# A hand-written order with decay columns made on TensorE against one annealed list of single steps, with Strassen's seven products in nine pairs

## The chip, the cores and the metric

The kernel runs on one core of one Trainium2 chip. The metric is the device time of one execution in microseconds (us). The core has a matrix engine (TensorE, PE in the profile; its weight loads are PEld), a vector engine (VectorE, DVE), an activation engine (ScalarE, ACT), a general engine (GpSimd, POOL) and a queue engine (SyncE, SP). Each works through its own instructions in order and waits on semaphores. TensorE writes to PSUM, eight banks of 128 x 512 float32.

## The reference

Two stages, float32 in and out. First a linear attention with decay for 4 batches, 8 heads, 768 tokens and head size 48, then a feed-forward layer of width 2048 on the 3072 tokens of 384 channels:

```python
for t in range(S):
    cur = einsum('bhd,bhe->bhde', u * k[t], v[t])
    y[t] = einsum('bhd,bhde->bhe', r[t], state + cur)
    state = w * state + einsum('bhd,bhe->bhde', k[t], v[t])
x = y.transpose(0, 2, 1, 3).reshape(3072, 384)
h = x @ w_in                      # 384 x 2048
out = maximum(0.01 * h, h) @ w_out   # 2048 x 384
```

## The kernel before

The tokens are cut into 24 stages of 128 (six to a batch), and two stages make a pair (12 pairs). A stage's attention is done in matrix form, the feed-forward layer stage by stage for the first four stages and pair by pair behind. Everything is bfloat16 in SBUF, with sums in PSUM. The steps have letters, which the lists and the texts use (n is a stage, m a pair):

- `r`, `k`, `v` n: loads of a stage, by DMA issued on POOL with a cast (L217); `wi`, `wo` g: quarters of w_in and w_out (L227, L231). Stage 0's r and k come over SP and ACT as float32.
- `P` n (prep): r and k times powers of the decay, on VectorE, from `qtab` and `ktab`, which ScalarE makes from w. From stage 8 on it also issues the transposition as a DMA on SP. `T` n (turn): for stages 0 to 7 the transposition as eight matmuls with `ident` (L367), copied out by ScalarE (L378).
- `A` n: the 128x128 products of r and k of all heads, two PSUM banks (L391). `M` n: their mask, on VectorE (L409; from stage DIAG on one predicated copy of 1024, L401, over the tile that `Q` laid out).
- The bonus u on the diagonal has two routes. Below stage DIAG (8): `X` n (VectorE, L329) and matmuls with `wu` inside `K` (L421), then `Q` scales v (L337), and three matmuls of `Y` add it (L513). From DIAG on: `Q` n computes one number per token and head with three VectorE operations (L342, L344, L346), and GpSimd multiplies `ident` by it into the two halves of `at` (L354).
- `K` n: the stage's update of the state (L425); below stage 8 the state carried over is added by a matmul with `ident` (L430), behind by VectorE in `S` (L478). `S` n: times the decay (L475, L480).
- `Y` n: attention output, from `at` and the state (L508), copied out as `xT`.
- `G` n.g, `J` m.j: parts of the first product for a stage (L541, four columns of blocks) or a pair (L558, two), each in one bank, with the leaky ReLU on ScalarE (L546, L564).
- `H` n, or `g2`: second product of a stage, 16 matmuls of 384 columns (L575). For pairs in SEVEN, `g2_seven` makes a pair's second product as Strassen's seven: seven times eight matmuls of 192 columns (L639), from four sums of halves of gT (`g_sum`, VectorE, L613) and of w_out (`w_sum`, L595). Products share banks: ScalarE keeps (`keep`, L647) and VectorE adds (`plus`, L670) between them.
- `C`, `W`: decay and bonus as columns. `C` turns the rows w and w*u by 16 + 8 one-column matmuls (L449, L450), ScalarE takes logarithms, VectorE casts `wu`; `W` makes the table `wl`. `U`: u over all partitions. `F` x: x matmuls of ones whose results nobody reads.

ORDER lists the steps up to pair 3 by hand, LOADS the first loads; then a loop over pairs 3 to 11 emits, for each pair, its first product, the attention of the stages two pairs on, and the second product of the pair before. Loads from stage 8 on wait for a J two pairs back (`pace`). Banks go round in the order of emission (`next_bank`).

Of the kernel before, what the change touches and what calls it, by code (L numbers as in the profile page):

```python
# [12 lines left out]
L = 128  # L13
# [10 lines left out]
FIRST, EARLY = 6, 2  # L24
LOADS = """r1 k1 r2 k2 wi0 id v1 r3 tri k3 v2 wi1 k4 r4 v3 wi2 k5 r5 r6 k6 v4 v5 k7 wi3 r7 v6 v7 wo3 wo2 wo1 wo0"""
ORDER = """
C W P0 P1 F1 T0 T1 P2 A0 X0 M0 A1 K0 T2 Q0 X1 Y0 A2 S0 M1 K1 X2 G0.0 Q1 P3 S1 Y1 T3 K2 M2 G1.0 X3 A3 U G0.1 S2 G1.1 Q2 M3 Y2 K3 P4
T4 Q3 G2.0 G2.1 G0.2 S3 G2.2 G1.2 Y3 P5 A4 P6 X4 M4 T5 X5 G3.0 K4 Q4 A5 S4 T6 G3.1 K5 G3.2 Y4 M5 L8 Q5 Y5 P7 A6 G1.3 J2.0 J2.1 T7
M6 X6 X7 K6 J2.2 J2.3 A7 S6 J2.4 J2.5 L9 Q6 G2.3 G0.3 J2.6 M7 L10 J2.7 L11 G3.3 K7 S7 P8 Q7 Q8 P9 H0 Q9 K8 H1 P10 L12 K9 H2 S8 S9
Y6 Y7 A8 A9 P11 M8 H3 M9 L13  # L30
# [90 lines left out]
def bass_rwkv5_eagle__then__act_leaky_relu_kernel(  # L121
# [17 lines left out]
    TURNED, DIAG = 8, 8  # L139
    SEVEN = (8,9,10,11)  # L140
# [17 lines left out]
    tcol = SB("tcol", [128, 1], FP32)  # L158
# [3 lines left out]
    wu_row = SB("wu_row", [1, HD])  # L162
# [6 lines left out]
    ku = [SB(f"ku{i}", [128, HD]) for i in range(2)]  # L169
    rku = [SB(f"rku{i}", [128, HD]) for i in range(2)]  # L170
    s_tok = [SB(f"s_tok{i}", [128, H], FP32) for i in range(2)]
# [5 lines left out]
    sum_t = [SB(f"sum_t{i}", [128, NP, 2 * D]) for i in range(2)]  # L177
# [41 lines left out]
    def load_stage(n, pace=()):  # L219
        for which in "krv":  # L220
            load_one(n, which, pace)
# [12 lines left out]
    def row(h):  # L234
# [5 lines left out]
    load_first("k")  # L240
    add("act", lambda: A.preload_act_table_set("natural_log_exp_and_others"))
    add("pool", lambda: G.iota(tcol[:, :], pattern=[[0, 1]], base=0, channel_multiplier=1,
                               allow_small_or_imprecise_dtypes=True), W=["tcol"])
    load_one(0, "v")
    add("dve", lambda: V.memset(one_row[:, :], 1.0), W=["one_row"])
    add("dve", lambda: V.memset(ones[:, :], 1.0), W=["ones"])
# [11 lines left out]

    ps_w, key_w = next_bank()

    def identity():
        add("pool", lambda: G.affine_select(ident[:, :], ones[:, 0:128], pattern=[[1, 128]], compare_op=ALU.is_equal,
                                            fill=0.0, base=0, channel_multiplier=-1), R=["ones"], W=["ident"])

    def triangle():
        add("pool", lambda: G.affine_select(mask[:, :], ones[:, 0:128], pattern=[[1, 128]], compare_op=ALU.is_ge,
                                            fill=0.0, base=-1, channel_multiplier=-1), R=["ones"], W=["mask"])

    for name in LOADS.split():
        if name == "id":  # L270
            identity()
        elif name == "tri":
            triangle()
        elif name[:2] == "wi":
            load_win(int(name[2:]))
        elif name[:2] == "wo":
            load_wout(int(name[2:]))
        else:
            load_one(int(name[1:]), name[0])

    add("dve", lambda: V.tensor_scalar(kexp[:, :], tcol[:, :], -1.0, float(MID - 1), ALU.mult, ALU.add),
        R=["tcol"], W=["kexp"])
    add("dve", lambda: V.tensor_scalar(qexp[:, :], tcol[:, :], 1.0, float(-MID), ALU.mult, ALU.add),
        R=["tcol"], W=["qexp"])
    add("dve", lambda: V.memset(v_sb[:, :, :].rearrange("p n (h e) -> p (n h) e", e=E)[:, :, D:E], 0.0), W=["v0"])
    add("dve", lambda: V.tensor_tensor(wu_row[:, :], w_row[:, :], u_row[:, :], ALU.mult),
        R=["w_row", "u_row"], W=["wu_row"])
# [11 lines left out]
    at_bank, kv_bank = {}, {}  # L299
# [10 lines left out]
    def prep(n):  # L310
        iq = n % NQK
        if n >= TURNED:
            both = rk_sb[:, n % NRK, :, :].rearrange("p w (h d) -> p (w h) d", d=D)
            by = tab[:, :, :].rearrange("p w (h d) -> p (w h) d", d=D)
            add("dve", lambda: V.tensor_tensor(qk[iq][:, :, 0:D], both, by, ALU.mult),
                R=[("r", n % NRK), ("k", n % NRK), "qtab", "ktab", ("qk0", iq)], W=[("qp", iq), ("kp", iq)])
            add("sp", lambda: SP.dma_start_transpose(tp[n % NTP][:, :, :],
                                                     qk[iq][:, :, :].rearrange("p h e -> p (h e)")),
                R=[("kp", iq), ("qp", iq), ("qk0", iq)], W=[("tp", n % NTP, 0), ("tp", n % NTP, 1)],
                dma=f"tp{n % NTP}")  # L320
            return
# [10 lines left out]
    def prep2(n):  # L332
        i2, iv = n % 2, n % NVS
# [7 lines left out]
        else:  # L341
            add("dve", lambda: V.tensor_tensor(ku[i2][:, :], k_of(n), u_tab[:, :], ALU.mult),  # L342
                R=[("k", n % NRK), "u_tab"], W=[("ku", i2)])
            add("dve", lambda: V.tensor_tensor(rku[i2][:, :], r_of(n), ku[i2][:, :], ALU.mult),  # L344
                R=[("r", n % NRK), ("ku", i2)], W=[("rku", i2)])
            add("dve", lambda: V.tensor_reduce(s_tok[i2][:, :], hd(rku[i2][:, :]), AX.X, ALU.add),  # L346
                R=[("rku", i2)], W=[("s", i2)])
            diag_tile(n)

    def diag_tile(n):  # L350
        ia = n % NAT
        for hh in range(2):
            s_of = s_tok[n % 2][:, :].rearrange("p (m two) -> p two m", two=2)[:, hh, :]
# [3 lines left out]
                R=["ident", ("s", n % 2)], W=[("at", ia, hh)])  # L357

    def turn(n):
        it, iq = n % NTP, n % NQK  # L360
        for half in ((0, 1) if n == 0 else (1, 0)):
# [12 lines left out]
            if n == 0 and half == 1:  # L374
                add("dve", lambda dst=dst, ps_t=ps_t: V.tensor_copy(dst, ps_t[:, :]),
                    R=[key], W=[("tp", it, half)])
            else:
                add("act", lambda dst=dst, ps_t=ps_t: A.activation(dst, ps_t[:, :], AF.Copy),  # L378
                    R=[key], W=[("tp", it, half)])

    def a_mm(n):
        it = n % NTP
        if n >= DIAG and taken[0] % 8 == 7:
            taken[0] += 1
# [12 lines left out]
    def a_mask(n):  # L397
        if n >= DIAG:
# [7 lines left out]
            return  # L406
        for hh in range(2):
            part = at_bank[n][hh][0][:, :].rearrange("p (m i) -> p m i", i=128)
            add("dve", lambda hh=hh, part=part: V.tensor_tensor(  # L409
                at[n % NAT][:, hh, :, :], part, mask[:, :].unsqueeze(1).to_broadcast([128, NP, 128]), ALU.mult),  # L410
                R=[at_bank[n][hh][1], "mask"], W=[("at", n % NAT, hh)])

    def kv_mm(n):
        iq = n % NQK
        ps_kv, key = kv_bank[n] = next_bank()
        live, carried = n % NC < NC - 1, n < DIAG and n % NC > 0
# [24 lines left out]
    def decay_columns():  # L441
        ps_c, key_c = next_bank()

        def emit():
            for hh in range(2):
                for p in range(NP):
                    c0 = (2 * p + hh) * D
                    rows = slice(64 * hh, 64 * hh + D)
                    PE.matmul(ps_c[rows, p:p + 1], w_row[:, c0:c0 + D], one_row[:, 0:1], start=True, stop=True)  # L449
                    last = PE.matmul(ps_c[rows, NP + p:NP + p + 1], wu_row[:, c0:c0 + D], one_row16[:, 0:1],  # L450
                                     start=True, stop=True)
            return last

        add("pe", emit, R=["one_row", "one_row16", "w_row", "wu_row"], W=[key_c, "wcols"])
        for hh in range(2):
            rows = slice(64 * hh, 64 * hh + D)
            add("act", lambda rows=rows, hh=hh: A.activation(wcol[rows, :], ps_c[rows, 0:NP], AF.Ln),
                R=[key_c], W=[f"wcol{hh}"])
            add("dve", lambda rows=rows, hh=hh: V.tensor_copy(
                wu[rows, :, hh:hh + 1].rearrange("p m o -> p (m o)"), ps_c[rows, NP:2 * NP]),  # L460
                R=[key_c, f"wcol{hh}", "wu"], W=[f"wu{hh}"])

    def decay_table():
        for hh in range(2):
            rows = slice(64 * hh, 64 * hh + D)
            add("act", lambda rows=rows, hh=hh: A.activation(
                wl[rows, :, hh * D:hh * D + D], wcol[rows, :].unsqueeze(2).to_broadcast([D, NP, D]), AF.Exp,
                scale=float(L)), R=[f"wcol{hh}", "wl"], W=[f"wl{hh}"])

    def state(n):  # L470
# [3 lines left out]
        if n % NC == 0 or n < DIAG:  # L474
            add("dve", lambda: V.tensor_tensor(new[:, :, :], kv, wl[:, :, :], ALU.mult),  # L475
                R=[key, "wl0", "wl1"], W=[("st", (n + 1) % NT)])
        else:
            add("dve", lambda: V.tensor_tensor(sum_t[n % 2][:, :, :], kv, st[n % NT][:, :, :], ALU.add),  # L478
                R=[key, ("st", n % NT)], W=[("sum", n % 2)])
            add("dve", lambda: V.tensor_tensor(new[:, :, :], sum_t[n % 2][:, :, :], wl[:, :, :], ALU.mult),  # L480
                R=[("sum", n % 2), "wl0", "wl1"], W=[("st", (n + 1) % NT)])
# [133 lines left out]
    def g2_seven(m):  # L615
        ig, i2 = m % NG, m % 2
        final = m == NST // 2 - 1
        banks = [next_bank() for _ in range(4 if final else 3)]
# [3 lines left out]
        def product(where, left, right, first, last):  # L622
            ps_o, key = banks[where]
# [19 lines left out]
            add("pe", emit, R=reads, W=[key])  # L643
# [30 lines left out]
        landed = []  # L674
        if not final:
            product(0, (0, 0), (top, one), True, False)
            keep(0, 0)
            product(1, 0, 0, True, False)
            keep(1, 1)
            product(0, 1, 1, False, False)  # L680
            keep(0, 2)
            product(2, (0, 1), (low, one), True, True)
            plus(2, 0, 0, 0)
            product(0, 2, 2, False, False)
            plus(0, 1, 1, 1)
# [132 lines left out]
```

## Time and profile before

| | |
|---|---|
| median of 3 runs | 171.15 us (171.03 to 171.33) |
| the profiled execution | 171.27 us, its span 169.5 us |
| TensorE busy | 163.1 us, 2203 matmuls |
| VectorE, ScalarE, GpSimd busy | 114.9, 93.3, 103.8 us |
| first product (L541, L558) | 13.0 and 54.5 us |
| second product plain, in sevens (L575, L639) | 43.3 us; 22.4 us in four groups |
| POOL-issued loads (queue q0) | 10.03 MB in 76512 packets |

The profile's span runs from the first instruction to the last; 1.77 us of the profiled execution's time lie around it. Busy times of TensorE count a matmul from its start to its modelled end, so neighbours overlap; start-to-start differences tell more. The chain of waits goes back from the last instruction to what released it.

### The profile page before, as it was taken

What the parts mean: (1) busy time and instruction counts of PE and PEld (TensorE: products, weight loads), DVE (VectorE), ACT (ScalarE), POOL (GpSimd) and SP (SyncE); (2) the same over time, 40 slices, a digit from 0 to 9 for tenths busy, and PEclk for the clock granted to TensorE, in tenths of its full rate; (3) what the DMA queues carried; (4) which work ended last, traced back from release to release, by engine and by line L of the source; (5) the groups of instructions that cost most, each with busy time, mean ns of one, the idle gap of its engine ahead of it and who ended that gap; (6) DMA issues with size and microseconds to landing.
All of it is one profiled execution on the core that took longest, in us unless ns stands there. A gap on an engine that the chain in (4) does not pass through costs nothing.

```text
span 169.5 us, 5112 instructions
## 1 busy us (share of the span) xinstructions
PE 163.1 (96%) x2203; PEld 129.1 (76%) x2203; DVE 114.9 (68%) x211; ACT 93.3 (55%) x176; POOL 103.8 (61%) x117
## 2 busy tenths in 40 slices
PE   6799999999999999999999999999999999999992
PEld 1577898889656876876866867867867899898991
DVE  7699766752998869379289299099199976053272
ACT  4752888789122852842933934824834836829320
POOL 7999999990379799791992995974506500000000
PEclk9999999999999999999999999999999999999999
DMA  5999999999999989999699499599107102011032
GB/s 95 117 155 159 170 155 171 194 185 145 126 167 197 167 50 126 214 73 114 172 74 156 130 74 154 135 106 205 51 0 173 48 4 93 4 40 55 4 115 70
DMA packets 99258, 19.66 MB, mean 116 GB/s; under 512 B 92322, under 2 KB 99236, under 8 KB 99236
## 3 DMA queue, kind: packets, MB, share of 16 engines
q0 software_dynamic: 76512, 10.03, 90.9%
q1 hardware_dynamic: 21682, 9.11, 25.6%
q8 instruction: 17, 0.28, 0.7%
q10 hardware_dynamic: 1042, 0.20, 0.6%
q14 instruction: 5, 0.04, 0.1%
HBM read 20.45 MB, written 4.72 MB: 148 GB/s over the span
## 4 chain that ended last, share of the span: by engine, by line
PE 93%; POOL 4%; ACT 1%; issue 1%; DVE 0%; DVEq 0%; POOLq 0%
PE ps_all L558 31%; PE ps_all L575 25%; PE ps_all L639 11%; PE ps_all L541 7%; PE ps_all L508 7%; PE ps_all L391 4%; PE ps_all L367 3%; PE ps_all L425 3%; POOL rk_sb L217 2%; PE ps_all L513 1%; ACT tp L378 1%; POOL v_sb L217 1%; PE ps_all L430 1%; PE ps_all L421 1%; POOL w_in_sb L227 0%
## 5 line engine op out<-in xcount | busy, mean ns | idle before, releaser
L558 PE MATMUL ps_all<-xT,w_in_sb 128*128 128x256 bf16 x480 | 54.5, 273 | 0.0
L354 POOL TENSOR_TENSOR at<-ident,s_tok 128x512 bf16<-128x512 bf16 x32 | 35.0, 1121 | 29.0 <-DVE s_tok L346 29.0
L558 PEld LDWEIGHTS ps_all<-xT,w_in_sb 128*128 128x128 bf16 x480 | 46.7, 98 | 6.1
L564 ACT ACTIVATE gT<-ps_all 128x512 bf16<-128x512 f32 x80 | 47.7, 597 | 5.8 <-PE ps_all L558 1.2
L575 PE MATMUL ps_all<-w_out_sb,gT 128*128 128x384 bf16 x256 | 43.3, 326 | 0.0
L575 PEld LDWEIGHTS ps_all<-w_out_sb,gT 128*128 128x128 bf16 x256 | 24.4, 98 | 15.9
L401 DVE CAST_PREDICATED at<-mask,ps_all 128x1024 bf16<-128x1024 uint16 x16 | 18.8, 1219 | 20.6 <-PE ps_all L391 20.6
L581 ACT ACTIVATE out_sb<-ps_all 128x384 f32<-128x384 f32 x16 | 7.8, 490 | 38.4 <-PE ps_all L575 38.4
L217 POOL DMA_DIRECT2D v_sb<-in_v_dram x24 | 22.6, 945 | 0.4 <-issue 0.4
L217 POOL DMA_DIRECT2D rk_sb<-in_k_dram x23 | 21.6, 941 | 0.0
L217 POOL DMA_DIRECT2D rk_sb<-in_r_dram x23 | 21.3, 929 | 0.0
L670 DVE TENSOR_TENSOR out_sb<-ps_all,snap 128x192 f32<-128x192 f32 x13 | 4.4, 355 | 15.1 <-PE ps_all L639 14.5
L344 DVE TENSOR_TENSOR rku<-rk_sb,ku 128x384 bf16<-128x384 bf16 x16 | 13.8, 861 | 0.6
L528 ACT ACTIVATE xT<-ps_all 128x384 bf16<-128x384 f32 x24 | 11.0, 490 | 5.1 <-PE ps_all L508 3.0
L541 PE MATMUL ps_all<-xT,w_in_sb 128*128 128x128 bf16 x192 | 13.0, 225 | 0.0
L541 PEld LDWEIGHTS ps_all<-xT,w_in_sb 128*128 128x128 bf16 x192 | 11.8, 101 | 0.5 <-issue 0.3
L409 DVE TENSOR_TENSOR at<-ps_all,mask 128x512 bf16<-128x512 f32 x16 | 10.2, 682 | 2.2 <-PE ps_all L391 2.2
L546 ACT ACTIVATE gT<-ps_all 128x512 bf16<-128x512 f32 x16 | 9.6, 599 | 3.8 <-PE ps_all L541 3.1
L508 PE MATMUL ps_all<-at,v_sb 128*32 128x128 bf16 x384 | 11.4, 228 | 0.0
L378 ACT ACTIVATE tp<-ps_all 128x512 bf16<-128x512 f32 x15 | 8.2, 596 | 3.7 <-PE ps_all L367 3.7
L508 PEld LDWEIGHTS ps_all<-at,v_sb 128*32 128x32 bf16 x384 | 8.4, 99 | 2.2 <-issue 0.5
L508 PE MATMUL ps_all<-tp,st 128*32 128x128 bf16 x240 | 9.8, 223 | 0.0
(80 smaller groups left out, 197.2 us busy)
## 6 DMA issues: line engine op xcount, KB each, us to landing
out_dram<-out_sb SPq DMA_DIRECT2D x22, 192.0 KB, 2.6
v_sb<-in_v_dram POOLq DMA_DIRECT2D x24, 96.0 KB, 5.5
rk_sb<-in_r_dram POOLq DMA_DIRECT2D x23, 96.0 KB, 5.2
rk_sb<-in_k_dram POOLq DMA_DIRECT2D x23, 96.0 KB, 4.6
w_in_sb<-in_moe_w_in_dram POOLq DMA_DIRECT2D x4, 384.0 KB, 7.0
w_out_sb<-in_moe_w_out_dram POOLq DMA_DIRECT2D x4, 384.0 KB, 10.9
out_dram<-out_sb SPq DMA_DIRECT2D x4, 96.0 KB, 1.7
tp<-qk SPq DMA_TRANSPOSE x16, 4.4
```

The lines of the kernel that those rows point to most:

```text
L217: add("pool", lambda: G.dma_start(dst, src), R=pace, W=[key], dma=f"{which}{n}")
L344: add("dve", lambda: V.tensor_tensor(rku[i2][:, :], r_of(n), ku[i2][:, :], ALU.mult), R=[("r", n % NRK), ("ku", i2)], W=[("rku", i2)])
L354: add("pool", lambda hh=hh, s_of=s_of: G.tensor_tensor(at[ia][:, hh, :, :], ident[:, :].unsqueeze(1).to_broadcast([128, NP, 128]), s_of.un ...
L401: add("dve", lambda: V.copy_predicated(at[n % NAT][:, :, :, :].rearrange("p two m i -> p (two m) i"), mask[:, :].bitcast(mybir.dt.uint16). ...
L409: add("dve", lambda hh=hh, part=part: V.tensor_tensor(at[n % NAT][:, hh, :, :], part, mask[:, :].unsqueeze(1).to_broadcast([128, NP, 128]) ...
L508: last = PE.matmul(ps_y[32 * q:32 * q + 32, 128 * s:128 * s + 128], a, m, start=first_mm and (s == 0 or n >= DIAG), stop=last_mm and n >= ...
L528: add("act", lambda: A.activation(xT[m % NX][:, :, 128 * half:128 * half + 128], ps_y[:, 0:HD].rearrange("p (s t) -> p s t", t=128), AF.Copy),
L541: last = PE.matmul(ps_g[:, 128 * f:128 * f + 128], w_in_sb[:, s, 128 * fb:128 * fb + 128], xT[ix][:, s, t], start=s == 0, stop=s == NSL - 1)
L558: last = PE.matmul(ps_g[:, 256 * f:256 * f + 256], w_in_sb[:, s, 128 * fb:128 * fb + 128], xT[ix][:, s, :], start=s == 0, stop=s == NSL - 1)
L564: add("act", lambda: A.activation(gT[ig][:, 2 * j:2 * j + 2, :].rearrange("p f t -> p (f t)"), ps_g[:, :], AF.Prelu, alpha=0.01), R=[key], ...
L575: last = PE.matmul(ps_o[:, 0:HD], gT[ig][:, s, 128 * half:128 * half + 128], w_out_sb[:, s, :], start=s == 0, stop=s == NFB - 1)
L639: done = PE.matmul(ps_o[:, 0:NH], lhs[:, s, :], rhs[:, s, :], start=first and s == 0, stop=s == HF - 1, skip_group_check=not (first and last))
```

## The change

The loop and LOADS go. One list, ORDER, names every load and every step; pairs' sums and products become single steps: `B` m.i a sum of gT, `V` i a sum of w_out, `Z` m.k a product of the seven with its keep, add or store. `I` x skips x banks. Loads have no pace. SEVEN holds pairs 3 to 11. DIAG goes from 8 to 6; the state is carried by a matmul for stages below CARRY (3) only. The decay and bonus columns come by four DMAs from w and u. `ident` and `mask` come from VectorE, from a ramp that POOL makes. `P` from stage 4 on is one operation for r and k. `M` n.how can take a half over ScalarE (bits 1, 2) or both halves in one operation (4). `ku` and `s_tok` have four buffers, `rku` is gone, the sums of states have four.

```diff
-FIRST, EARLY = 6, 2
-LOADS = """r1 k1 r2 k2 wi0 id v1 r3 tri k3 v2 wi1 k4 r4 v3 wi2 k5 r5 r6 k6 v4 v5 k7 wi3 r7 v6 v7 wo3 wo2 wo1 wo0"""
+EARLY = 3
 ORDER = """
-C W P0 P1 F1 T0 T1 P2 A0 X0 M0 A1 K0 T2 Q0 X1 Y0 A2 S0 M1 K1 X2 G0.0 Q1 P3 S1 Y1 T3 K2 M2 G1.0 X3 A3 U G0.1 S2 G1.1 Q2 M3 Y2 K3 P4
...
+wi0 r1 I3 F4 F2 I4 P0 I4 k1 C v0 r2 k2 T0 I1 r3 k3 v1 k5 v2 I4 F2 P1 A0 W r5 T1 X0 M0.4 F2 P2.0 K0 U Q0 T2 S0 A1 Y0 P3.0 X1 wi3 T3 X2 k4 A2 v3 r4 I3 r7 k7 M1.4 wi2 K1 wi1 S1 Q1 G0.0 k6 r6 v4 I3 I4 I4 K2 P5 Q2 M2.1 A3 M3.3 X3 Y1 T5 I3 G0.3 S2 Y2 G1.0 K3 P4 Q3 G1.3 T4 S3 v6 G2.3 v5 G2.0 Y3 k8 r8 P7 X5 A4 Q7 M4.0 A5 X4 G2.2 G3.2 wo3 wo0 M5.2 G3.3 v7 wo1 G1.1 wo2 Q6 G3.1 G0.2 T7 K4 G2.1 Q4 G1.2 Y4 P6 K5 S4 Q5 T6 G3.0 Y5 A7 A6 G0.1
...
+Q8 K7 r11 k10 I4 Y6 r10 Y7 k11 I2 v9 J2.0 S7 P8 J2.1 v10 k13 k12 r16 r12 J2.7 V0 V2 J2.2 P9 V1 J2.5 H3 K8 V3 S8 H0 P10 H1 H2 Q9 J3.0 A9 P11 A8 K9 Q10 Q11 J3.5 M9 J3.1 J3.2 J3.4 I4 v13 r14 v12 r17 r20 J3.3 M8 J3.7 r15 v11 P13 K10 P12 Y8 Y9 S9 A10 Q13
...
+B3.0 r21 M11 A12 M13 v16 Y11 B3.1 Y10 I1 Y13 J4.0 J5.2 B3.2 M12 K13 J5.4 Y12 J5.5 Q16 S13 J4.1 P16 J5.0 P14 P15 J4.3 v14 Z3.0 J5.6 J6.1 k18 J6.0 J5.1 J4.4 k21 r18 k19 I3 Q14 J5.7 P17 K14 r19 B3.3 A16 A14 Q15 Z3.1 I1 J4.5 S14 M16 v15 J5.3 Z3.2 M14 Q17 Z3.3 J6.3 Z3.4 A15 M15 I1 A17 Z3.5 Z3.6 J6.4 B4.0 J6.7 Y15 M17 Y14 J6.5 J6.6 B5.0 K15 K16 Z5.0 P18 Z5.1
...
+Z4.6 J7.0 P19 B6.2 B6.0 J7.4 J7.6 M18 J7.1 K19 B6.1 Q20 v21 Q19 J7.5 J7.3 J8.2 J8.1 J7.2 P23 P22 S19 J7.7 I3 Z6.0 B6.3 J8.3 Y18 A19 Z6.1 M19 Z6.2 J8.5 Z6.3 Z6.4 I1 B7.0 Z6.5 Z7.0 Z6.6 Y19 B7.1 B7.3 A20 B7.2 Z7.1 J9.1 Q21 Z7.2 K20 M20 Z7.3 Z7.4 Z7.5 A21 J8.4 S20 J8.6 Z7.6 J8.0 M21 J9.5 Q22
...
+J10.5 Z10.0 B11.2 J11.5 Z9.5 Z9.6 B10.0 B10.1 B11.0 B11.1 Z11.0 Z11.1 Z10.1 Z11.2 B11.3 B10.3 Z11.3 Z11.4 Z10.2 Z11.5 Z10.3 Z10.4 Z10.5 Z11.6 Z10.6 I3
 """
...
-    TURNED, DIAG = 8, 8
-    SEVEN = (8,9,10,11)
+    TURNED, DIAG, CARRY = 8, 6, 3
+    SEVEN = (3, 4, 5, 6, 7, 8, 9, 10, 11)
...
+    for hh in range(2):
+        for name, src, dst in (("wcol", w, wcol), ("ucol", u, ucol)):
+            add("sp", lambda src=src, dst=dst, hh=hh: SP.dma_start(
+                dst[64 * hh:64 * hh + D, :], dram(src, hh * D, [[1, D], [2 * D, NP], [1, 1]]), allow_slow_non_contiguous=True),
+                W=[f"{name}{hh}"], dma=f"{name}{hh}")
...
+    add("dve", lambda: V.tensor_scalar(ident[:, :], ramp[:, :], 0.0, None, ALU.is_equal), R=["ramp"], W=["ident"])
...
-    def prep(n):
+    def prep(n, how=0):
         iq = n % NQK
-        if n >= TURNED:
+        if n >= 4 or how:
...
-    def a_mask(n):
+    def a_mask(n, how=0):
...
+            if (how >> hh) & 1:
+                raw, half = at[n % NAT][:, hh, :, :], ("at", n % NAT, hh)
+                add("act", lambda raw=raw, part=part: A.activation(raw, part, AF.Copy),
+                    R=[at_bank[n][hh][1]], W=[half])
+                add("dve", lambda raw=raw: V.tensor_tensor(
+                    raw, raw, mask[:, :].unsqueeze(1).to_broadcast([128, NP, 128]), ALU.mult),
+                    R=["mask", half], W=[half])
+                continue
...
-        live, carried = n % NC < NC - 1, n < DIAG and n % NC > 0
+        live, carried = n % NC < NC - 1, n < CARRY and n % NC > 0
...
-    def g2_seven(m):
+    def g2_seven(m, k):
...
+            if k == 0:
+                product(0, (0, 0), (top, one), True, False)
+                keep(0, 0)
+            elif k == 1:
+                product(1, 0, 0, True, False)
+                keep(1, 1)
+            elif k == 2:
+                product(0, 1, 1, False, False)
+                keep(0, 2)
+            elif k == 3:
+                product(2, (0, 1), (low, one), True, True)
+                plus(2, 0, 0, 0)
+            elif k == 4:
+                product(0, 2, 2, False, False)
+                plus(0, 1, 1, 1)
+            elif k == 5:
+                product(1, 3, (low, two), False, True)
+                plus(1, 2, 0, 1)
+            else:
+                product(0, (1, 1), 3, False, True)
+                plain(0, 1, 0)
...
```

In the file the new list stands on one line.

## The prediction

> **What bounds the kernel now.** I read the engine shares, then the chain of waits, then the chain in order of time, and last single rows of TensorE and VectorE.
>
> ```profile
> PE 163.1 (96%) x2203; PEld 129.1 (76%) x2203; DVE 114.9 (68%) x211; ACT 93.3 (55%) x176; POOL 103.8 (61%) x117
> ...
> PE 93%; POOL 4%; ACT 1%; issue 1%; DVE 0%; DVEq 0%; POOLq 0%
> ```
>
> TensorE (PE) is busy for 163.1 of 169.5 us and is 93% of the chain that ended last. VectorE (DVE) has room, 115 of 169.5. So a change is worth what it takes off TensorE, unless it makes TensorE wait.
>
> ```profile
> 6.72 0.54 POOL ident L262
> 7.30 1.57 PE ps_all L367 x12
> 8.90 1.09 ACT tp L378 x2
> ...
> 14.42 1.28 PE ps_all L541 x12
> ...
> 17.70 0.67 PE ps_all L541 x12
> ...
> 98.94 5.20 PE ps_all L575 x32
> 104.14 5.24 PE ps_all L558 x48
> ...
> 135.94 4.68 PE ps_all L639 x56
> ```
>
> The columns are start, us, what. TensorE's useful work begins at 7.30. The same twelve matmuls take 1.28 at 14.4 and 0.67 at 17.7: TensorE runs at half speed until about 16 (the page's PEclk line shows 9 in every slice and hides it). From then on it is dense: a pair's second product is 5.20 plainly (L575) and 4.68 as seven products (L639), start to start.
>
> I add up TensorE's work at full speed from the first transposition (T0) to the last product, with start-to-start times of the trace: T 0.447, A 0.330, Y 0.506 (0.339 for a sequence's first stage), four g1 columns 0.67, one J 0.655, a plain second product of one stage 2.60, one of seven 0.667, K 0.17, its diagonal part 0.104, its carried part 0.163, Y's diagonal part 0.22. Before this is 153.4. Clock minus work done I call TensorE's lag. At 16.48, with 4.45 done, it is 12.0; when the last product ends, at 166.13, it is 12.7. The head loses 12.0 us and the 150 us behind it only 0.7. The change can gain in two places only: the work, and the head.
>
> **TensorE's work.** Five more pairs (3 to 7) as seven products: 5 x (5.20 - 4.68) = 2.6. CARRY 3 drops K's carried matmul for stages 3, 4, 7: 3 x 0.163 = 0.5. DIAG 6 drops both diagonal parts for stages 6, 7: 2 x (0.104 + 0.22) = 0.65. Together 3.74, leaving 149.7. The first products, A and T stay in number. The decay columns (24 tiny matmuls, 4.18 to 5.72) lie ahead of T0 beside ScalarE's tables and are worth nothing by themselves.
>
> **The head.** P0 (VectorE) waited behind the casts of the decay columns until 6.54; qtab was ready at 5.49. In the new order P0 can start at 5.55 and T0 near 6.2. The six fills F4 F2 ahead of T0, at half speed 0.43 each from about 4.3, can hold it to 6.9. Neither sets the pace: the next wait is stage 1's keys. In the trace the POOL-issued loads land one after another, 0.7 apart, v0 at 5.94, r1 6.66, k1 7.39, and wi0 needs 2.4 (the w_out pieces 1.95). The list puts wi0 first and v0 behind k1, so k1 lands at 7.39 - 0.70 + 1.95 to 2.4 = 8.6 to 9.1, and up to 9.6 with the four column DMAs (not in this trace; they need 4-byte elements, bounded by 0 and 0.5). I take 8.8. From there VectorE's in-order queue sets the pace: P1 ends at 9.15 with 1.41 of its work done; with M0 as one 1024-wide product (1.22 by L401, 1.36 as two of L409; I take 1.36) its lag is 7.85. Two places decide. Y2 needs M2, 10.92 of VectorE work: 10.92 + 7.85 + 0.2 = 19.0, with 7.59 of TensorE work ahead of it: lag 11.4. Y5 needs Q5, 24.3 (Q6 and Q7 at 1.26 free plus 0.4 of collisions): 32.3 against 21.13: lag 11.2. I take 11.3: a gain of 0.7. Bounds: k1 at 8.2 and 1.22 per mask give 10.6, k1 at 9.6 gives 12.1. Halves of M2, M3 and M5 go over ScalarE (0.60 each, L378's size); its 23.2 of work up to T6 plus 1.0 of tables from about 7.5 end near 32, in time for A6.
>
> **Behind the head.** VectorE gains 20 sums (L613, 0.69 alone, 1.41 beside a GpSimd tile; mean 0.79): 15.9; 15 adds of 0.356: 5.3; stages 6 and 7 by the token route, 2 x (1.82 - 0.42 - 0.55): 1.7; three carried states: 1.2. It goes from 115 to about 138 us. ScalarE gains 15 keeps and 5 plain copies of 0.33, loses 10 of 0.49, gains 4 masks: some 4 us, beside TensorE. GpSimd gains 4 tiles of 1.08. The order spreads VectorE's work evenly. Its tightest place: J8.6 takes a PSUM bank that the add of Z7.5 frees. VectorE has 112.4 up to that add, TensorE 110.25 up to J8.6: 112.4 + 7.85 = 120.2 against 110.25 + 11.3 = 121.5, spare 1.3. Other tight places, by the same difference from one wait to the next (S14 to M20, S14 to M18, M9 to M10), are from 0.2 spare to 0.7 short. I charge 0.5 for them (0 to 2.5), and for the lag's drift the same 0.7 as before: A behind J costs 0.096 more, as at 60.1 in the trace, in six places (0.6), and neighbouring Ys save 0.05 each in eight (0.4).
>
> **Queues passed.** The loads lose their pace waits and stand in the POOL queue between tiles. Issued every 0.87, they run ahead of use, except r10: POOL's sum puts its issue at 42 to 44, landing 3.3 later, so P10 (due 44 to 46) can stall VectorE by about 1.2, which 1.6 spare at Y8 hides. On SP, P18's transposition (4.4 us, at worst 6.5) has some 6 us before A18, P14's and P16's six and a half; P19's stands behind the four stores of pairs 4 and 5, whose last copy ends near 102, and A19 is due near 110. I charge nothing; without that cover it is up to 2 each.
>
> **The end.** Last is Z10.6: a ScalarE copy (0.2 + 0.33), then a 192 KB store (2.6 by the DMA issues) against the last 96 KB store (1.7) issued 1.0 after the last matmul: 3.1 against 2.7, +0.4 (0 to 0.9).
>
> **Sum.** The profiled execution took 171.27 (span 169.5, 1.77 around it): 171.27 - 3.74 (work) - 0.7 (head) + 0.5 (ties) + 0.4 (end) = 167.7. It lies 0.12 above the median of the three runs, so 167.6 for a median.
>
> **Rivals.** *V, VectorE becomes the bound (slower).* In the trace VectorE's products of two SBUF operands stand still beside GpSimd's tiles:
>
> ```profile
> 54.80 0.36 DVE L344 TENSOR_TENSOR rku<-rk_sb,ku 128x384 bf16<-128x384 bf16 x1
> ...
> 56.04 2.23 DVE L344 TENSOR_TENSOR rku<-rk_sb,ku 128x384 bf16<-128x384 bf16 x1
> ...
> 131.56 1.41 DVE L613 TENSOR_TENSOR gs<-gs,gT 128x1024 bf16<-128x1024 bf16 x1
> ...
> 151.85 0.69 DVE L613 TENSOR_TENSOR gs<-gs,gT 128x1024 bf16<-128x1024 bf16 x1
> ```
>
> The columns are start, us, what. The same product takes 0.36 free and 2.23 with two tiles running (GpSimd, 55.94 to 58.04); the same sum takes 0.69 free and 1.41 beside one. All 20 new sums lie between Q13 and Q23, where the tiles run. If each takes 1.41 instead of the 0.79 I charged, VectorE is 12.4 later; less the spare 1.3, TensorE ends 11.1 later: 178.7. It decides from about eight such sums (8 x 0.62 > 3.5 + 1.3). For it: three of the four sums that met tiles were slowed. Against: VectorE has 138 of some 166; my means already hold 14 us of such collisions; and after most Qs the list places masks, states or adds that read PSUM, which the tiles do not slow (L401 1.225 beside a tile, 1.218 alone). Chance 0.15, at 172 to 178.
>
> The Trainium skill, SBUF — State Buffer, section "SBUF: two separate sides", says that VectorE with two SBUF inputs and GpSimd hold a shared port pair in turn, for a whole instruction, the other fully blocked. The trace agrees (1.41 and 2.23). By that rule every new sum that meets a tile waits for up to one tile, 1.08 here, which gives this rival's 178.7 if all meet one.
>
> *C, the clock stays at half speed into the order's thin stretch.* T3 to A3 then take 5.3 instead of 2.7 in the 3.8 us before Y1, the first products behind them double as well: lag 13 to 14, 169.3 to 170.3. For it: before, full speed came only at 16, after some 3.5 us without gaps. Against: nine fills ahead of T0 instead of three keep TensorE busy from 1.5 to about 7, and four more stand in the gaps behind it. Chance 0.10.
>
> The Trainium skill, TensorE: Matmul & The Clock Gate, section "What's actually happening", says that the gate opens after a busy, free-running window of about 3.4 us; the trace's 1.28 and 0.67 agree. By it the fills should open the gate before stage 1, at 5 to 8.5 (an estimate from that page).
>
> *Q, queues.* Two or three of the transpositions and loads above come late: +2.5 to +4, 170 to 171.7. For it: before, transpositions took up to 6.5 when loads stood in the rings. Chance 0.12.
>
> *B, better.* k1 early, no ties, the end at no cost: 171.27 - 3.74 - 1.4 - 0.5 = 165.6, and 164.9 if the drift of 0.7 goes too. Chance 0.13.
>
> That the change isn't what it says is excluded: the list names all seven parts for pairs 3 to 11, 63 products against 28.
>
> **Numbers.** Forecast 167.6, by itself 166 to 169: 0.50. A measurement of this kernel tells about 0.2% (0.35 us). Faster: 0.50 + 0.13 + 0.10 and 0.05 of Q: 0.78; within 0.2%: 0.05; slower: the rest of Q and V, 0.17. The range 164.8 to 171.6 leaves out nearly all of V and a sliver below.
>
> **What would show it.** After: 504 matmuls of 128x192 at L650, and 96 of L575's 256 left (now L578); TensorE's first dense stretch near 19 with lag 11.3; twelve g1 matmuls in 0.67 already behind Y0; PE idle after 35 us under 2 us. Wrong if PE waits for the sums (L616), adds or masks of VectorE by more than 3 us in total behind 40 us (V), if the first group of L544 takes 1.28 (C), or if A waits on DMA tp (Q).

## The result: slower by 2.7%, and the profile after

The changed kernel takes 175.94 us (median of four runs, 174.77 to 177.91) against 171.12 beside it: ratio 1.027, interval 1.0232 to 1.0307. The forecast was 167.6. The profiled execution is the slowest of the four: its mean granted clock is 0.981, the others ran at 0.990, 0.990 and 1.000 and took 176.50, 175.37 and 174.77. Medians in this text are of all runs of a kernel; the ratios leave out slow runs (over 1.5% above the kernel's fastest), without which the medians would be 175.37 for this kernel, 177.26 for e4, 170.37 for e7, 175.81 for e8, 169.89 for e10 and 172.58 for e11.

The page of the changed kernel: engines, granted clock, chain by engine, two DMA issues (KB each, median us from issue to landing).

```profile
PE 163.0 (93%) x2292; PEld 135.8 (77%) x2292; DVE 136.7 (78%) x243; ACT 96.5 (55%) x191; POOL 106.6 (61%) x119
...
PEclk9999999999999999999759999999999999999999
...
PE 44%; DVE 20%; DMA 18%; POOL 13%; issue 3%; ACT 0%; DVEq 0%; POOLq 0%; ACTq 0%
...
rk_sb<-in_r_dram POOLq DMA_DIRECT2D x23, 96.0 KB, 6.4
...
tp<-qk SPq DMA_TRANSPOSE x16, 6.0
```

The same two DMA rows before:

```profile
rk_sb<-in_r_dram POOLq DMA_DIRECT2D x23, 96.0 KB, 5.2
...
tp<-qk SPq DMA_TRANSPOSE x16, 4.4
```

TensorE is as busy as before (163.0 against 163.1 us) but its share of the chain falls from 93% to 44%: VectorE, DMA and POOL took the rest. The clock row, all 9 before, has a 7 and a 5 in its middle. A transposition lands 6.0 us after its issue (4.4 before), a load of r 6.4 (5.2).

The waits of the changed kernel (total us, times, longest), and its chain in order of time (start, us, what):

```profile
DVE qk L313 <- DMA rk_sb<-in_r_dram: 5.2, 3, 1.9
PE ps_all L388 <- DMA tp<-qk: 4.5, 3, 2.7
...
PE ps_all L438 <- DMA v_sb<-in_v_dram: 1.2, 1, 1.2
```

```profile
48.37 10.92 DMA rk_sb<-in_r_dram
59.39 0.56 DVE qk L313
...
78.91 7.53 DMA tp<-qk
86.57 0.61 PE ps_all L388 x8
...
99.17 7.34 DMA tp<-qk
106.64 0.40 PE ps_all L388 x8
```

The rows name three places. The load of r12, issued at 48.37, lands at 59.29; VectorE waits for it in P12, in order, with S9, Q13, S10, Q12 and M10 behind it: H5 is held by S9 and A11 by M10. Ahead of M10 three of VectorE's operations also stood still beside GpSimd's tiles: they took 0.84, 1.24 and 1.08 (0.36, 0.35 and 0.36 free). K12 itself waits for v12, 1.2. The transposition of P14, issued at 78.91, lands at 86.44 and A14 waits 2.7 us for it; that of P18, 99.17 to 106.5, holds A18 up 1.5. The stretch around A14 beside a dense one of the same kernel (stretch, length, then busy time and instructions of PE, PEld, DVE, ACT, POOL; granted clock, DMA share, GB/s):

```profile
83.00:93.00 10.00, 6.94 (x56) 5.66 (x54) 6.36 (x9) 2.43 (x5) 7.83 (x9) 0.66 1.40 121
124.00:160.00 36.00, 36.00 (x518) 32.75 (x517) 25.53 (x46) 20.48 (x41) 6.38 (x6) 1.00 0.17 43
```

In the ten us from 83 TensorE is busy for 6.94 at a clock of 0.66 (the clock's record says half from 85.5 to 92.3); from 124 on it is busy for all of 36. The prediction's lag (clock less work done at full speed) puts figures on it: 11.7 at 26 us; +0.6 at J3.4 (56); +3.3 in three places from 60 to 67 (H5, K12, A11: r12 and v12); +0.4 at A16 and +2.8 at A14; +2.65 while the clock is half; +1.5 at A18; +0.6 at J8.5. It ends at 23.5, where the forecast had 12.5 (11.3 and 1.2 for ties and drift).

### The profile page after: what moved, and what is told of

The parts are those of the page before. It is cut to its first block, busy times and chain, and to the rows that moved or that the text cites. A ratio compares the mean times of both kernels' runs of the same rounds, so it can differ in the third digit from the quotient of the medians.

```text
span 176.1 us, 5345 instructions
## 1 busy us (share of the span) xinstructions
PE 163.0 (93%) x2292; PEld 135.8 (77%) x2292; DVE 136.7 (78%) x243; ACT 96.5 (55%) x191; POOL 106.6 (61%) x119
## 3 DMA queue, kind: packets, MB, share of 16 engines
q0 software_dynamic: 76512, 10.03, 91.3%
## 4 chain that ended last, share of the span: by engine, by line
PE 44%; DVE 20%; DMA 18%; POOL 13%; issue 3%; ACT 0%; DVEq 0%; POOLq 0%; ACTq 0%
PE ps_all L650 20%; PE ps_all L561 13%; DMA rk_sb<-in_r_dram 10%; DMA tp<-qk 8%; POOL rk_sb L213 8%; DVE at L398 5%; DVE qk L313 5%; PE ps_all L544 4%; POOL v_sb L213 3%; PE ps_all L388 2%; PE ps_all L511 2%; DVE ku L345 2%; DVE gs L616 2%; DVE ku L343 2%; DVE s_tok L347 1%
## 5 line engine op out<-in xcount | busy, mean ns | idle before, releaser
L567 ACT ACTIVATE gT<-ps_all 128x512 bf16<-128x512 f32 x80 | 47.8, 597 | 22.9 <-PE ps_all L561 20.0
L561 PEld LDWEIGHTS ps_all<-xT,w_in_sb 128*128 128x128 bf16 x480 | 46.3, 99 | 7.5 <-DVE at L398 0.7
L650 PE MATMUL ps_all<-tw,gs 128*128 128x192 bf16 x216 | 22.4, 255 | 0.0
L650 PEld LDWEIGHTS ps_all<-tw,gs 128*128 128x128 bf16 x216 | 18.7, 101 | 1.0 <-issue 0.2
L658 ACT ACTIVATE snap<-ps_all 128x192 f32<-128x192 f32 x27 | 8.9, 331 | 19.2 <-PE ps_all L650 18.8
L313 DVE TENSOR_TENSOR qk<-rk_sb,tab 128x768 bf16<-128x768 bf16 x20 | 15.4, 781 | 5.2 <-DMA rk_sb<-in_r_dram 5.2
L578 PE MATMUL ps_all<-w_out_sb,gT 128*128 128x384 bf16 x96 | 16.3, 326 | 1.0 <-DVE sum_t L481 1.0
L616 DVE TENSOR_TENSOR gs<-gT 128x1024 bf16<-128x1024 bf16 x18 | 13.5, 759 | 3.1 <-ACT gT L567 3.1
L650 PE MATMUL ps_all<-w_out_sb,gT 128*128 128x192 bf16 x144 | 14.7, 246 | 0.0
L388 PE MATMUL ps_all<-tp 48*128 48x128 bf16 x192 | 9.1, 225 | 5.2 <-DMA tp<-qk 4.5
L544 PE MATMUL ps_all<-xT,w_in_sb 128*128 128x128 bf16 x192 | 12.4, 219 | 0.4 <-issue 0.4
L650 PEld LDWEIGHTS ps_all<-w_out_sb,gT 128*128 128x128 bf16 x144 | 12.3, 99 | 0.2
```

The costliest lines, as they stand in the source:

```text
L388: last = PE.matmul(at_bank[n][hh][0][:, 128 * p:128 * p + 128], tp[it][rows, NP + p, :], tp[it][rows, p, :], start=True, stop=True)
L544: last = PE.matmul(ps_g[:, 128 * f:128 * f + 128], w_in_sb[:, s, 128 * fb:128 * fb + 128], xT[ix][:, s, t], start=s == 0, stop=s == NSL - 1)
L561: last = PE.matmul(ps_g[:, 256 * f:256 * f + 256], w_in_sb[:, s, 128 * fb:128 * fb + 128], xT[ix][:, s, :], start=s == 0, stop=s == NSL - 1)
L567: add("act", lambda: A.activation(gT[ig][:, 2 * j:2 * j + 2, :].rearrange("p f t -> p (f t)"), ps_g[:, :], AF.Prelu, alpha=0.01), R=[key], ...
L578: last = PE.matmul(ps_o[:, 0:HD], gT[ig][:, s, 128 * half:128 * half + 128], w_out_sb[:, s, :], start=s == 0, stop=s == NFB - 1)
L616: add("dve", lambda: V.tensor_tensor(x[i][:, :, :], a, b, op), R=keys, W=[("gs", m % 2, i)])
```

## Experiments

Theory Q: the list's loads and transpositions are issued too few microseconds ahead of their users. Theory V: VectorE, standing still beside GpSimd's tiles, has no time for the 20 new sums. The waits given are TensorE's idle times; what a place "loses" is what the lag grows by there, which is some 0.1 more.

### e1: loads in the order of their first users

```diff
-... r9 k9 r13 v8 k16 r11 k10 r10 k11 v9 v10 k13 k12 r16 r12 v13 r14 v12 ...
+... r9 k9 v8 k10 r10 r11 k11 v9 r13 k13 v10 k12 r12 v12 v11 v13 k16 r16 ...
```

(Only the loads of the list are shown. They keep their places in it and change names; everything else stays.)

> The list of after, with the 46 loads from stage 9 on in the same places of the list but in the order in which their first users stand (k12 and r12 seven loads earlier, r16, k16, r20, r17 later). Theory Q (loads and transpositions land late): r12 lands before its P12 is due at about 56 us, the lag stays near 12.5 up to A11 where after had 15.6, and the time falls by 2 to 4 us to 171 to 174. Theory V (VectorE beside GpSimd's tiles is the bound): no operation of VectorE is taken away, so the time stays within 1 us of after, 174.5 to 177. Theory C (the half clock): it goes only if the wait at A14 goes; if that stays, 1 us at most.

174.64 us (174.34 to 175.19), 1.3 less. At A11 the lag is 13.4 in place of 15.6: the loss between 55 and 67 us is gone. A16 and A14 still wait (0.8 and 2.1), the clock is half for 3.4 us, A18 waits 1.3. The time lies in V's range and outside of Q's, 171 to 174: Q was right on the place (A11) and wrong on what it is worth. The runs of the two kernels overlap (the changed one starts at 174.77), so the gain is read from the lag. Late loads are a part, and the smaller one.

### e2: loads with few packets

```diff
+        if n >= 8 and which != "v":
+            src = dram({"k": k, "r": r}[which], n * L * HD, [[HD, L], [D, H], [1, D]])
```

(From stage 8 on r and k are read from contiguous rows, which are other values than the reference's.)

> The list of after, but from stage 8 on r and k are read from contiguous rows of 384 numbers (the right number of bytes from other places, so the values of these stages are not the reference's): 128 packets a load in place of 1024. All waits, tiles and engine operations stay. Theory Q: the DMA engines are nearly free behind 45 us, r12 and the transpositions land in time, the lag stays at 12 to 13.5 to the end, time 166.5 to 169. Theory V: same VectorE and GpSimd work, so within 1.5 us of after, 174 to 177.

178.91 us (178.07 to 179.77). The POOL queue falls from 76512 packets to 47840, its share of the DMA engines from 91.3% to 65.7%, and r12 lands at 54.9. But the transposition still takes 5.9 (median) and P14's 79.14 to 87.03: A14 waits 2.9. v12, issued at 57.99 behind the tiles of Q9 to Q11, lands at 64.85 and K12 waits 2.2. The clock is half for 10.2 us in all. So fewer packets heal r12 alone, and the time is far from Q's 166.5 to 169 and above V's range too.

### e3: the nine pairs without the list

```diff
-    SEVEN = (8,9,10,11)
+    SEVEN = (3, 4, 5, 6, 7, 8, 9, 10, 11)
...
-        if 4 <= m < 8:
-            w_sum(m - 4)
+        if m == 3:
+            for i in range(4):
+                w_sum(i)
```

(In the kernel before.)

> The kernel before with one change: seven products in pairs 3 to 11 instead of 8 to 11 (the four sums of w_out all in the loop's first turn). The order by pairs, DIAG 8, the paces stay. By TensorE's work alone 171.1 - 2.6 = 168.5. Theory V: a turn of the loop then has 11.8 us of TensorE work against VectorE's 9.1 + 4.2 and collisions, so VectorE sets the turn for pairs 4 to 8 and the time is 172 to 177. Theory Q: the sevens themselves are harmless, 168.5 to 170.

179.86 us (179.22 to 180.24). This order does a pair's seven products and their sums in one go; the lag grows from 12.5 at 50 us to 23.6 at 154, most of it at the products. The longest of TensorE's waits behind the head:

```profile
PE ps_all L639 <- DVE at L401: 7.7, 6, 2.7
```

That is VectorE: six waits of products, 7.7 us, for a bank that a mask has to free. Before the longest (74.3 to 77.0 us) the mask stands behind four sums in a row, 71.4 to 75.8, of which two took 1.42. The time is above V's range (172 to 177). So V is real where the sums stand in a row, and the list spreads them.

### e4: matmuls that fill the wait

```diff
-... B3.3 A16 A14 ... B4.1 A18 ...
+... B3.3 A16 F6 A14 ... B4.1 F6 A18 ...
```

> The list of after with six matmuls of ones (1.3 us at full speed) ahead of A14 and of A18, the two places where TensorE waited for a transposition. Theory C: the half clock behind A14 (6.8 us of it in the profiled run of after, 2.7 us lost) does not come, time down by 1.5 to 3 us, 172.5 to 174.5. Theories Q and V: the wait itself stays as long; if the half clock comes anyway, the time is that of after or up to 1 us more.

177.49 us (175.36 to 178.97). In the profiled run the clock stays open at 85 but is half at 68.6 to 72.0, after a wait of 3.7 at K12 for v12. A14 comes no sooner: the fills' 1.3 and 0.7 of waiting stand in the wait's place, and the lag still grows by 2.6 there. The time is above what any of the theories had. A fill doesn't bring a transposition sooner, and the gap that closes the clock can be another one.

### e5: three transpositions earlier

```diff
-... B3.2 M12 K13 J5.4 Y12 J5.5 Q16 S13 J4.1 P16 J5.0 P14 P15 J4.3 ...
+... B3.2 M12 K13 J5.4 Y12 J5.5 P14 P16 Q16 S13 J4.1 J5.0 P15 J4.3 ...
-... Z3.6 J6.4 B4.0 J6.7 Y15 M17 Y14 J6.5 J6.6 B5.0 K15 K16 Z5.0 P18 Z5.1 ...
+... Z3.6 J6.4 P18 B4.0 J6.7 Y15 M17 Y14 J6.5 J6.6 B5.0 K15 K16 Z5.0 Z5.1 ...
```

(On top of the loads in the order of their users. As P14 now uses its loads earlier, a few of them change places again: r14 and k14, k18, r18, v15 and v16.)

> The loads of e1_need_order, and three steps moved ahead in the list: P14 and P16 (product and DMA transposition) to just ahead of Q16, P18 to just ahead of B4.0; the loads again stand in the order of their first users. TensorE's own sequence is that of the changed kernel. Theory Q (the list gives the transpositions too few microseconds between VectorE's product and the A that reads them): the waits of A16 and A14 (together 3.4 us of lag in e1), the half clock behind them (1.6) and the wait of A18 (1.3) all go, and TensorE ends 5 to 6 us earlier: 168.5 to 170. Theory V (VectorE, slowed beside GpSimd's tiles, has no time for the sums): VectorE's work is the same and only its order changes, so a mask, a state or a sum is late in place of the transposition, and the time stays within 1 of e1's 174.6.

168.90 us (168.76 to 169.28) against 170.86 beside it: ratio 0.9882, interval 0.9853 to 0.9911. Faster than both kernels, from the place of three steps and of the loads. Its page and its chain in order:

```profile
PE 159.3 (95%) x2292; PEld 133.4 (80%) x2292; DVE 136.2 (81%) x243; ACT 96.5 (58%) x191; POOL 106.7 (64%) x119
...
PE 59%; DVE 22%; DMA 8%; issue 5%; POOL 3%; ACT 3%; DVEq 0%; POOLq 0%; ACTq 0%
...
tp<-qk SPq DMA_TRANSPOSE x16, 6.9
```

```profile
73.46 0.70 PE ps_all L561 x6
74.15 7.67 DMA tp<-qk
81.95 0.62 PE ps_all L388 x16
```

The transpositions are no quicker (6.9); P14 and P16 are issued at 71.9 and 74.2 instead of 78.9 and 77.6, and what is left is 1.0 at A16. The clock does not close behind a wait (granted 1.000), A18 waits for nothing. The time is in Q's range. The lag ends at 14.9 instead of 23.5.

### e6: plain second products in pairs 3 to 7

```diff
-... J4.3 r18 Z3.0 J5.6 J6.1 r21 J6.0 ... r20 B3.3 A16 A14 Q15 Z3.1 ... M14 Q17 Z3.3 J6.3 Z3.4 ... Z3.5 Z3.6 J6.4
+... J4.3 r18 I1 J5.6 J6.1 r21 J6.0 ... r20 A16 A14 Q15 I1 I1 ... M14 Q17 H6 J6.3 ... H7 I7 J6.4
```

(The same in pairs 4 to 7, and no B3.i to B7.i. The plain products take banks out of turn, so the values of some stages are changed.)

> The loads of e1_need_order, and the second products of pairs 3 to 7 in the plain form (H) in place of the seven: the 20 sums (B) and 15 adds of these pairs are gone, TensorE gets 2.6 us more work, and the plain products' bank order can cost some waits on ScalarE's copies behind 90 us (each up to 0.9). Three of the removed sums stood ahead of P14 and P16 on VectorE (3.4 to 4.5 us of it). Theory V: with the sums gone VectorE reaches P16 and P14 early, A16 and A14 wait for nothing, the clock does not close, A18 waits for nothing: lag some 6 less, 171 to 173. Theory Q: P16 and P14 stand behind S13, which waits for TensorE's K13 anyway, so A16 and A14 still wait 2.5 to 3.5 together for transpositions that are issued less than 8 us ahead of them: 176 to 179.

182.47 us (181.18 to 182.99): further off than either theory had it, because the banks cost losses of 0.3 to 0.8 in eight places behind 87 us. What it was made for is ahead of them: with all sums gone A16 and A14 wait 1.2 and 2.1, no less than with them (0.8 and 2.1 in e1). Against V, as far as it reaches.

### e7: every VectorE step reordered

```diff
-... r9 k9 K6 v8 M7 k10 M6 ... J2.7 V0 V2 J2.2 P9 V1 J2.5 H3 K8 V3 S8 H0 P10 H1 H2 Q9 J3.0 A9 P11 A8 K9 Q10 Q11 J3.5 M9 ...
+... P8 r10 r11 r9 M7 K6 ... J2.7 v10 V0 S7 k11 V2 J2.2 r17 V1 J2.5 P9 H3 K8 V3 r12 H0 r13 H1 P10 H2 J3.0 k16 v11 Q10 k12 Q9 S8 A9 v12 Q11 P11 A8 r16 M9 ...
```

> From e5_early_turns, with the steps P, Q, M, S and B and the loads put into another order from stage 9 on, chosen so that with the measured durations (a sum or product of two SBUF operands standing still beside a GpSimd tile, 6 us for a transposition, 2.1 for issuing one behind another) no TensorE step waits; TensorE's sequence, all work on every engine and the number of each step stay those of the changed kernel. Theory Q (order and distances only): lag stays at the head's 12.3 to the end as the prediction had it, 166.5 to 168.5, below the kernel before. Theory V (VectorE's capacity): no order helps, over 173.

170.41 us (169.60 to 172.59), ratio 0.9987 (0.996 to 1.0014). Behind 68 us the lag grows by 0.9 only, so Q's half holds there; the front failed. The loads had been moved ahead as well, and P9 and P10 wait 1.9 and 0.6 for them, a state takes 3.0 beside tiles (0.36 free), and J3.4 loses 2.0 to M9, which stands behind; the clock is half from 59.0 to 62.4. The time is in neither range (Q 166.5 to 168.5, V over 173).

### e8: the early transpositions with the changed kernel's loads

(The two moves above, and the loads as the change has them.)

> The changed kernel with its own order of loads, and only P14 and P16 moved to just ahead of Q16 and P18 to just ahead of B4.0 (the other half of e5_early_turns). If the two causes stand side by side (late loads 1.3, late transpositions 5.7 by e1 and e5): 175.9 - 5.7 = 170.2. If they hang together (P12 still waits for r12 on VectorE's in-order queue, so VectorE reaches P14 late wherever the list puts it, and K12 and K14 wait for v12 and v14): the early place is worth little, 173 to 176, and the gain of e5 needs both.

176.29 us (174.73 to 177.74): no gain. P14 stands earlier in the list and is issued at 79.0 all the same (74.2 in e5), because a mask ahead of it on VectorE waits 1.6 for an A of TensorE, which K12 has held up. With no load in flight for P16 and one for P14 they take only 3.3 and 3.1, so A16 and A14 wait for nothing. The loss is elsewhere: K12 waits 3.7 for v12, which POOL issues behind six tiles, the clock is half from 69.8 to 73.2, Z4.6 loses 1.8 and J8.5 1.3. The two causes do not add up singly:

| | P14, P16, P18 as changed | early |
|---|---|---|
| loads as changed | 175.94 | 176.29 |
| loads by first user | 174.64 | 168.90 |

### e9: the sums behind the transpositions

```diff
-... k18 B3.0 M11 ... Y11 B3.1 Y10 ... J5.2 B3.2 M12 ... P16 J5.0 P14 P15 J4.3 ...
+... M11 ... Y11 Y10 ... J5.2 M12 ... P16 J5.0 P14 P15 B3.0 B3.1 B3.2 J4.3 ...
```

(On top of the loads in the order of their users.)

> e1_need_order with one thing changed: the three sums B3.0, B3.1 and B3.2, which stood ahead of P14 and P16 on VectorE, behind P15. All the work is the same. Theory V (the sums make VectorE late): P16 and P14 are done 3 us or more earlier, A16 and A14 wait for less than 0.5 together, the clock stays open, 170 to 172. Theory Q (the list puts P16 and P14 behind S13, which VectorE can only do once TensorE's K13 is through): they are done less than 1.5 us earlier, A16 and A14 still wait 1.5 to 3 together, and the sums now make Z3.1 to Z3.3 later: 173.5 to 176.5.

173.60 us (173.22 to 174.05). A16 and A14 still wait 1.1 and 1.5 (0.8 and 2.1 in e1), the clock is still half for 3.4 us. Q's case; the sums ahead of P14 cost 1.0 us in all.

### e10: VectorE's steps again, loads left alone

```diff
-... Q9 J3.0 A9 P11 A8 K9 Q10 Q11 J3.5 M9 ... H5 S10 J3.6 K12 J4.6 J4.2 r17 Q12 M10 S12 A11 ...
+... Q9 Q11 J3.0 A9 A8 P11 K9 M9 J3.5 ... Q10 ... S10 H5 J3.6 Q12 K12 J4.6 M10 J4.2 r17 A11 S12 ...
```

> e5_early_turns with VectorE's steps (P, Q, M, S, B) reordered from Q9 on, mostly by a few places (Q11 ahead of Q10, M9 ahead of Q10, P14 and P16 ahead of M12 and S13); the loads stay in the order and nearly at the places of e5, and TensorE's sequence is that of the changed kernel. In e7 the loads had been moved ahead too, and the dense early loads came late themselves. Theory Q (places only): the four remaining losses of e5 (J3.4 0.6, A11 0.5, A16 1.05, J8.5 0.4) shrink to under 1 together: 167.0 to 168.3. Theory V (VectorE, which stands idle nowhere between 38 and 87 us in e5, is the bound in this stretch): what one user gains another loses, 168.5 to 170.

170.07 us (169.32 to 172.84), ratio 0.9933 (0.9906 to 0.996): 1.2 above e5. J3.4, A16 and J8.5 are healed, but two new places at 85 and 87 us lose 0.4 and 0.7 and A11 loses 1.9, as VectorE's rows before M10 show (start, us):

```profile
62.90 1.19 DVE L343 TENSOR_TENSOR ku<-rk_sb,u_tab 128x384 bf16<-128x384 bf16 x1
64.12 1.28 DVE L345 TENSOR_TENSOR ku<-rk_sb,ku 128x384 bf16<-128x384 bf16 x1
...
65.91 1.21 DVE L398 CAST_PREDICATED at<-mask,ps_all 128x1024 bf16<-128x1024 uint16 x1
```

Q12's two products take 1.19 and 1.28 beside tiles, where they take 0.35 and 0.36 free, and the mask M10 stands behind them. Here V's mechanism decides, by 1.8 us at one place. V's price, 168.5 to 170, is all but met.

### e11 and e12: tiles of 16 columns

```diff
-                at[ia][:, hh, :, :], ident[:, :].unsqueeze(1).to_broadcast([128, NP, 128]),
-                s_of.unsqueeze(2).to_broadcast([128, NP, 128]), ALU.mult),
+                at[ia][:, hh, :, 0:16], ident[:, 0:16].unsqueeze(1).to_broadcast([128, NP, 16]),
+                s_of.unsqueeze(2).to_broadcast([128, NP, 16]), ALU.mult),
```

> e1_need_order, with GpSimd's diagonal tiles 16 of 128 columns wide (the bonus of the other columns is left out): 0.15 to 0.2 us in place of 1.05, so VectorE's products and sums hardly meet them. All other work and the list stay. Theory V (VectorE slowed beside the tiles): VectorE wins 10 us or more over the kernel, A16, A14 and A18 wait for nothing, the clock stays open, and TensorE has about the head's lag of 12.3 to the end: 167 to 169. Theory Q (the distance in the list): P16 and P14 still stand behind S13, which needs TensorE's K13; they come at most 3 us earlier, A16 and A14 still wait 1 to 3 together: 171 to 174.

173.45 us (171.29 to 175.60). A tile takes 0.34 in place of 1.1, and VectorE's busy time falls by 15.6 us (136.8 in e1). The page, the waits and the chain in order:

```profile
PE 161.0 (94%) x2292; PEld 135.1 (79%) x2292; DVE 121.2 (70%) x243; ACT 96.5 (56%) x191; POOL 79.3 (46%) x119
```

```profile
DVE sum_t L481 <- PE ps_all L438: 6.1, 6, 2.4
...
PE ps_all L388 <- DMA tp<-qk: 5.0, 3, 2.3
```

```profile
75.03 8.08 DMA tp<-qk
...
93.11 8.17 DMA tp<-qk
```

VectorE now waits itself, for K's sums among others (6.1 us), and A still waits 5.0 for transpositions that take 8.1 and 8.2. With VectorE unburdened the changed list is still slower than the kernel before (1.0089, from 1.0049), and the time is in Q's range. So V isn't the main cause. The run does not free VectorE alone: GpSimd has less to do too and issues the loads sooner. P14 was issued 3.1 us earlier than in e1 (75.0 against 78.1), but took 8.1 in place of 6.0 and landed only 1.0 earlier. Had it kept its 6.0, A14 would hardly have waited, so what VectorE's standing still costs at A14 stays open.

> e5_early_turns with the same small tiles (16 of 128 columns; the bonus of the others left out). It bounds what VectorE's standing still beside the tiles still costs there: the four losses left (J3.4, A11, A16, J8.5; 2.5 us of lag). Theory V for these: they go, 166.5 to 167.3. If they are places in the list or transpositions: 168 to 169.

(The same tiles on e5.) 168.40 us (168.05 to 169.69), 0.5 below e5, in the range for places and transpositions. The one wait of TensorE over 0.25 us behind 28 us is A11's, 1.0, for a transposition. So little is left to V there.

## Why the prediction was wrong, by its steps

**Queues passed: the step that failed.** It charged nothing for the transpositions of P14, P16 and P18 and nothing for late loads ("without that cover it is up to 2 each"). Two things were off. The duration: it took 4.4, "at worst 6.5", from a trace in which loads were paced. In the changed list they have no pace; the transpositions of P14 and P18 took 7.5 and 7.3, and up to 8.5 in e5. That the loads beside them make them long is likely, not shown by a run of its own: in e8, with no load or one in flight, P16 and P14 took 3.3 and 3.1, but e2's fewer packets did not shorten them. The cover: for P14 "six and a half" us were forecast; A14 was otherwise ready at 83.85, 4.9 after P14's issue. P18 had its six. r10's stall came as charged (P10 waits 1.8 against 1.2); it and 2.3 us that three of VectorE's products lost beside tiles between 49 and 55 us were hidden but for 0.6 at J3.4. r12, tenth in a row of loads on POOL's queue, has no term; it took 10.9. Before, loads late in a row took up to 12.7 too, but VectorE waited for r only 0.9 in all.

**What no step had: the clock can close again.** The prediction weighs the clock in the head only (rival C). In the changed kernel it fell to half for 3.4 or 6.8 us around a wait, +2.65 in the profiled run. Its four runs therefore spread over 3.1 us, where the prediction had 0.35 us for what a measurement can tell. Rival C itself did not come: the first twelve products of L544 stand 0.056 us apart, at full speed, where the first of L541 stood 0.107 apart before.

**Rival Q** had the mechanism and the places, with a chance of 0.12 and a price of 2.5 to 4; e5 against the changed kernel shows 7.0. It missed that the places hang together: a late r12 or v12 holds up TensorE or VectorE's queue, what stands behind is issued later, and a long wait closes the clock on top. The table of four shows that neither the loads nor the transpositions alone bring the gain.

**Rival V**'s span, 172 to 178, holds the result by luck. Its condition was some eight sums slowed beside tiles, and the sums of the changed kernel (shortest/median/longest in ns) show three of 36, at 1.21 to 1.53 us, the others at 0.68 or 0.69:

```profile
L616 DVE TENSOR_TENSOR gs<-gT x18: 678/682/1529, 67.8 to 165.7; 128x1024 bf16<-128x1024 bf16 x18
L616 DVE TENSOR_TENSOR gs<-gs,gT x9: 677/684/692, 71.2 to 166.5; 128x1024 bf16<-128x1024 bf16 x9
L616 DVE TENSOR_TENSOR gs<-gT,gs x9: 681/683/1534, 80.1 to 168.4; 128x1024 bf16<-128x1024 bf16 x9
```

TensorE never waits for a sum; for masks it waits 1.1 us. What VectorE's instructions took above the shortest of their kind adds up to 18.6 us (12.0 before), of which the sums have 2.5; most of it falls on Q's products, on preps and on states. VectorE has 136.7 us of work (138 forecast, though its terms add up to 139), the sums 0.75 each (0.79).

**The terms that held.** TensorE's work: 504 matmuls of 192 columns; in e5, where most of the waits are gone, 171.27 - 3.74 (work) + 2.2 (lag 14.9 against 12.7) - 0.6 (end) is 169.1, and its profiled run took 169.28. The head: k1 lands at 8.55 (8.8 forecast), the lag is 10.8 to 11.2 near 20 us (11.3 forecast). But a pause of TensorE near 26 us, for which the profile names no releaser, takes most of it back (0.5 in the changed kernel, 0.8 in e5): there the lag is 11.7 and 12.3 (before, 12.2), so the gain of 0.7 held only in part. The end went the other way: from the last product's end to the end of the span it is 2.8 us after and 3.4 before, -0.6 where +0.4 was charged. Ties and drift: 1.2 charged, 2.5 in e5, of which 1.0 is A16's wait for a transposition.

**The lines to watch.** "PE idle after 35 us under 2 us" did not hold: the eight waits from 55 us on add up to 8.1. "Wrong if ... A waits on DMA tp (Q)" is the row that shows it, 4.5 us. The rows for V (over 3 us of waits for sums, adds or masks) and for C did not appear.

## What to carry to other kernels

In a list that is filled to the brim, ask of every DMA how long it takes in the new company, not in the old, and how many microseconds of the consumer's work the list puts between issue and use; a median over the old list says little there. Move the issue first and the engines' work last: here three steps and the order of loads were together worth 7 us (175.94 to 168.90) and neither alone more than 1.3, while freeing VectorE of 15 us was worth 1.2 on the changed list with its loads sorted (174.64 to 173.45) and 0.5 on e5. A gap in TensorE's work can cost twice, by its length and by the clock behind it.

## What the runs showed of the hardware that was not expected

- The clock closes in the midst of a dense kernel. Waits of 0.3 and 2.7 us within four us (the changed kernel), 0.8 and 2.1 (e1), 1.1 and 1.5 (e9), or single ones of 3.7 (e4, e8), 2.2 (e2) and 2.3 (A18 of e11) went with 3.4 or 6.8 us at half speed; single ones of 2.2 (A14 of e11), 1.8 (e10) and 1.4 (A18 of the changed kernel) did not. The same program closed it in three of four runs. The Trainium skill, TensorE: Matmul & The Clock Gate, section "What's actually happening", names a free-running window of some 3.4 us, idle or busy: the steps of 3.4 and 6.8 and the differences between runs agree, but waits shorter than a window, some of them split in two, closed it here.
- A DMA transposition's issue takes SP 1.23 to 1.46 us alone and 2.1 to 2.65 behind another (the changed kernel). From issue to landing it took 3.2 to 6.5 us in the kernel before, up to 9.4 with unpaced loads beside it (e12), and 3.7 to 4.8 from 109 us on in the changed kernel, where one load at most is in flight beside each. Fewer packets (e2) did not shorten it (median 5.9 against 6.0).
